# Hashed attention and a GELU feed-forward on one core: the second pair's feature transfers split between two queues, the weights' conversion shifted by one pair, the last accumulator in another PSUM bank

## The chip, the core and the metric

The kernel runs on one core of a Trainium2 chip. The metric is the device time of one execution in microseconds, the median of five runs. Beside it stands one profiled execution, with a record of every instruction of every engine; all times of single instructions below are from that execution, counted from its first instruction.

## What is computed

```python
q, k, v: (4, 8, 768, 64)     proj: (64, 6)     w_in: (512, 2048)     w_out: (2048, 512)
q_bits = (q @ proj > 0);  k_bits = (k @ proj > 0)        # 6 hash bits for each query and key
mask   = bucket(q_bits) == bucket(k_bits)
scores = where(mask, q @ k.T / 8, -1e9)
attn   = softmax(scores) @ v                             # (4, 8, 768, 64)
x      = attn.transpose(0, 2, 1, 3).reshape(3072, 512)
h      = x @ w_in
out    = (h / (1 + exp(-1.702 * h))) @ w_out             # (3072, 512)
```

All inputs and the output are float32; the two weights arrive as float64 and the kernel converts them bit by bit on the chip.

## The kernel before

**Two stages.** Attention takes about the first 328 us, the feed-forward the rest. The feed-forward multiplies by a block scheme with 7 products for 8 in two levels, so it needs sums of quarters of the weights (`in_sums`, on GpSimd) and of x (`x_sums`, on VectorE) before its first products. Four engines (TensorE, VectorE, ScalarE and GpSimd) execute in the order in which the program is written. SyncE only issues transfers; its order is chosen by the scheduler, which may move a transfer up past others when nothing it depends on holds it. Transfers signal through eight counters in turn, so an issue also waits for the transfer that used its counter before.

**Attention in pairs.** The 32 heads are handled as 16 pairs n = 0 to 15, two heads side by side in the 128 partitions. Each pair has two column halves c = 0 and 1 of 384 queries. One round of the main loop is one (n, c), called here by those numbers (pair 0 has its halves split once more). In a round TensorE computes `scores` of (n, c), six key tiles of 128, each with a masking product of the features `kf`, `qf` and a product of `kT`, `qT` (L432), into one of three two-bank PSUM buffers `ps`. ScalarE exponentiates each (L433), which frees its buffer. In the same round TensorE multiplies the round before's exponentials by the values (`values`, L456) into the accumulator `av`, which ScalarE unloads (L467, L468). `av` is one PSUM bank of the pool `aps`, and a second one-bank pool `mps`, tag "m", holds in turn the hashes, the denominators `dn` and the row of `guard`.

**Preparing the next pair.** In the rounds with c = 0 VectorE transposes the next pair's k and q as they have come from memory (`turn`, L391), ScalarE takes their squares' sum (`measure`, L398), TensorE hashes them (`hashed`, L408), and `featured` compares on VectorE (L413, tile `f`) and copies pieces of `f` into `kf` and `qf` by eight transfers of 9 KB (L420). For pair 1 four of these eight are issued by ScalarE and four by SyncE, for all others SyncE issues all eight. The raw k and q of a pair come in by eight transfers of 96 KB (`fetch`, L328) in pieces of 128 bytes.

**Denominators.** Exponentials are added up by GpSimd (`add_low`, L440, L441) and VectorE (`add_high`, L446, L448); TensorE sums over partitions (`total`, L477), VectorE inverts (`invert`, L484 to L492) and scales (`norm`, L497).

**Weights' conversion.** `w_in` comes in 16 chunks of 512 KB (L162, tile `raw`, one buffer). Fourteen are converted inside attention, one for a pair, two in the feed-forward. A conversion has three VectorE steps in the round with c = 0 (L178, L182, L186), one ScalarE step (L190, square), and three VectorE steps in the round with c = 1 (L193, L195, L198). `begin(n)` starts the generator and issues its load at the end of round (n-1, 1).

**The end of attention.** `guard(0)` reduces the sizes to one column on VectorE (L520), `guard(1)` turns it on TensorE (L523, tile `row`, in the bank "m") and reduces the row on VectorE (L524). In the kernel before, `guard(0)` stands in round (15, 1) and `guard(1)` after the last `values`.

Of the kernel before, what the change touches and what calls it, by code (L numbers as in the profile page):

```python
# [8 lines left out]
F32 = mybir.dt.float32  # L9
# [10 lines left out]
P = 128  # L20
# [18 lines left out]
def kernel(  # L39
# [17 lines left out]
    nc = tc.nc  # L57
# [10 lines left out]
    HS = HT * P  # L68
# [84 lines left out]
    for x in (0x3FFFFFFF, 0xFF800000):  # L153
        m = const.tile([P, 1], U32, name=f"mask_{x:x}")
# [3 lines left out]
    def convert(cv, dst, src, queue=None, psum=None):  # L158


        raw = cv.tile([P, CW, 2], U32, tag="raw", name="raw")
        (queue or loader[0]).dma_start(out=raw, in_=src)  # L162

        def of(x):
            return x if len(dst.shape) == 2 else x.rearrange("p (x r) -> p x r", r=dst.shape[2])

        lo, hi = raw[:, :, 0], raw[:, :, 1]
        bits = cv.tile([P, CW], U32, tag="bits", name="bits")
        if psum is None:
            part, size = dst.bitcast(U32), hi.bitcast(F32)  # L170
        else:
            part = psum.tile([P, CW], U32, tag="part", name="part")
            size = psum.tile([P, CW], F32, tag="size", name="size")
        yield


        if psum is None:
            nc.vector.scalar_tensor_tensor(part, hi, 3, masks[0x3FFFFFFF], op0=Alu.logical_shift_left, op1=Alu.bitwise_and)  # L178
        else:
            nc.vector.tensor_scalar(part, hi, 3, 0x3FFFFFFF, op0=Alu.logical_shift_left, op1=Alu.bitwise_and)  # L180
        yield
        nc.vector.scalar_tensor_tensor(bits, hi, 0xC0000000, part, op0=Alu.bitwise_and, op1=Alu.bitwise_or)  # L182
        yield

        if psum is None:
            nc.vector.tensor_tensor(part, bits, masks[0xFF800000], op=Alu.bitwise_and)  # L186
        else:
            nc.vector.tensor_scalar(part, bits, 0xFF800000, None, op0=Alu.bitwise_and)

        nc.scalar.activation(size, hi.bitcast(F32), Act.Square)  # L190
        part = part.bitcast(F32)
        yield
        nc.vector.scalar_tensor_tensor(part, lo, 2.0**-52, part, op0=Alu.mult, op1=Alu.mult)  # L193
        yield
        nc.vector.tensor_tensor(dst, of(bits.bitcast(F32)), of(part), op=Alu.add)  # L195
        yield

        nc.vector.scalar_tensor_tensor(dst, of(size), (1.125 * 2.0**-15) ** 2, dst, op0=Alu.is_ge, op1=Alu.mult)  # L198
# [3 lines left out]
    in_chunks = [(w_in_sb[:, kc, f : f + CW], wi[kc, :, f : f + CW])  # L202
                 for f0 in range(0, FF // 2, CW) for f in (f0, FF // 2 + f0) for kc in range(KC)]


    LATE = 2
# [76 lines left out]
    def attention(ff):  # L283
# [4 lines left out]
        with actx:  # L288
            ld = actx.enter_context(tc.tile_pool(name="ld", bufs=1))
            wk = actx.enter_context(tc.tile_pool(name="wk", bufs=2))  # L290
            cv = actx.enter_context(tc.tile_pool(name="cv", bufs=1))
            st = actx.enter_context(tc.tile_pool(name="st", bufs=2))
            aps = actx.enter_context(tc.tile_pool(name="aps", bufs=1, space=PSUM))
            mps = actx.enter_context(tc.tile_pool(name="mps", bufs=1, space=PSUM))
# [93 lines left out]
            def turn(n, name):  # L388
                x = raws[n, name]
                xt = xts[n, name] = wk.tile([P, S], F32, tag=f"{name}T", name=f"{name}T")  # L390
                nc.vector.transpose(xt, x.rearrange("p s i -> p (s i)"))  # L391
# [19 lines left out]
            def featured(n):  # L411
                f = wk.tile([P, HS], BF16, tag="f", name="f", bufs=1)
                nc.vector.tensor_scalar(f, dots.pop(n), above[:, 0:1], weight[:, 0:1], op0=Alu.is_gt, op1=Alu.mult)  # L413
                for c in range(2):
                    for i, x in enumerate("kq"):

                        queue = nc.scalar if (n, x) == (1, "q") else nc.sync
                        for j in range(2):
                            r0 = D * i + 32 * c + 2 * NB * j
                            queue.dma_start(out=feats[n % 2][x][D * j : D * j + 2 * NB, c * HS : (c + 1) * HS],  # L420
                                            in_=f[r0 : r0 + 2 * NB, :])
# [13 lines left out]
            accs, avs = {}, {}  # L435

            def add_low(n, c):

                acc = accs[n, c, 0] = st.tile([P, 2, HS], F32, tag="acc0", name="acc0", bufs=1)
                nc.gpsimd.tensor_tensor(acc, es[c][:, 0, :, 0:HS], es[c][:, 1, :, 0:HS], op=Alu.add)  # L440
                nc.gpsimd.tensor_tensor(acc, acc, es[c][:, 2, :, 0:HS], op=Alu.add)  # L441
# [7 lines left out]

            def values(n, c, kts):  # L450
                if 0 in kts:
                    avs[n, c] = aps.tile([P, HS + 1], F32, tag="av", name="av")
                av, vt = avs[n, c], vts[n]
                for t in kts:
                    for j in range(2):
                        nc.tensor.matmul(av[D * j : D * (j + 1), :], vt[:, t, j, :], es[c][:, t, j, :],  # L456
                                         start=(t == 0), stop=(t == T - 1))
# [37 lines left out]
            def norm(n):  # L495
# [4 lines left out]
            groups = [(n, c, kts) for n in range(len(pairs)) for c in range(2)  # L500
                      for kts in ((range(GT), range(GT, T)) if n == 0 else (range(T),))]
            last = len(pairs) - 1
            conv = {}

            def step(n, count=1):
                for _ in range(count):
                    next(conv.get(n, iter(())), None)

            def begin(n):
                if n - 1 < len(in_chunks) - LATE:  # L510

                    conv[n] = convert(cv, *in_chunks[n - 1], nc.sync if n > 1 else nc.scalar)
                    step(n)


# [2 lines left out]
            def guard(part):  # L518
                if part == 0:
                    nc.vector.tensor_reduce(largest, sizes, axis=AX.X, op=Alu.max)  # L520
                else:
                    row = mps.tile([1, P], F32, tag="m", name="row")
                    nc.tensor.transpose(row, largest, ident)  # L523
                    nc.vector.tensor_reduce(largest[0:1, 0:1], row, axis=AX.X, op=Alu.max)  # L524
# [7 lines left out]
            for g in range(len(groups) + 2):  # L532
                n, c, kts = groups[g] if g < len(groups) else (last + 1, 0, ())
                prev = groups[g - 1] if 1 <= g <= len(groups) else None
                if kts:
                    scores(n, c, kts)
                    if g == 0:
                        rest()
                    if kts[0] == 0:
                        add_low(n, c)  # L540


                if hashes:
                    featured(hashes.pop())
                ended = prev and prev[2][-1] == T - 1
                if ended:
                    add_high(*prev[:2])
                    if prev[1] == 1:
                        totals.append((g + (g == len(groups)), prev[0]))

                turned = ("", "k", "q", "")[g] if n == 0 else "kq" if c == 0 and n < last else ""
                for x in turned:
                    turn(n + 1, x)
                    measure(n + 1, x)
                while norms:
                    norm(norms.pop(0))
                if totals and totals[0][0] == g:
                    norms.append(totals.pop(0)[1])
                    total(norms[-1])
                    invert(norms[-1])  # L560
                if prev:
                    values(*prev)
                if ended:
                    unload(*prev[:2])
                if "q" in turned:
                    hashed(n + 1)
                    if n:
                        hashes.append(n + 1)
                    else:
                        featured(n + 1)  # L570
                    for x in "kq":
                        if n + 2 <= last:
                            fetch(n + 2, x)
                    fetch_v(n + 1)
                if kts and kts[-1] == T - 1:
                    step(n, 3)
                    if c == 0 and n > last - len(x_sums):
                        x_sums[n - last - 1]()
                    if c == 1:
                        begin(n + 1)  # L580
                if g == len(groups) - 1:
                    guard(0)
                if g == len(groups):
                    guard(1)
                    for f in in_sums(0):
                        f()
                    early.close()
                    next(ff)
# [410 lines left out]
```

## Time and profile before

| | |
|---|---|
| median of 5 runs | 884.34 us (884.04 to 884.95) |
| profiled execution | 884.37 us, span from first to last instruction 882.5 us |
| granted TensorE clock | 0.996 |
| busy, share of the span | TensorE 866.5 us (98%), VectorE 724.5 us (82%), ScalarE 313.4 us (36%), GpSimd 320.3 us (36%) |
| chain that ended last | 97% TensorE |
| TensorE waits on another engine | ScalarE exponential 2.5 us in 2 waits, unload of `av` 0.9 us in 1, later unloads 1.0 us in 2 |

The busy rows count the time in which an engine had an instruction under way. The chain is followed back from the last instruction to what released it, so its shares say which engine set the time. A timeline row reads: start, duration, engine, line, operation, output<-inputs, count; in brackets the idle time before it and what ended that. Rows marked SPq and ACTq are the issuing of transfers by SyncE and ScalarE.

### The profile page before, as it was taken

The numbers are of one execution on the slowest core, as the hardware profiler recorded it, in microseconds if no ns is written. First come the engines' busy times: TensorE is split into PE (matmuls) and PEld (weight loads), VectorE is DVE, ScalarE is ACT, GpSimd is POOL, SyncE is SP. The second block draws the span as 40 slices with busy tenths as digits, with TensorE's granted clock in tenths as the row PEclk, the third lists the DMA queues.
The fourth block names the chain that finished last, engine by engine and source line by source line (L and its number), as shares of the span: only waits on it lengthen the run. The fifth ranks groups of instructions, "written<-read, shape, count | busy, mean of one in ns | idle before, by whom it ended". The sixth has DMA issues, their size and how long they took to land.

```text
span 882.5 us, 11926 instructions
## 1 busy us (share of the span) xinstructions
PE 866.5 (98%) x4077; PEld 497.4 (56%) x4077; DVE 724.5 (82%) x1020; ACT 313.4 (36%) x519; POOL 320.3 (36%) x275
## 2 busy tenths in 40 slices
PE   9899999999999999999999999999999999999995
PEld 4444444444444444444444444444888888888884
DVE  4599999999999956777777887888898977897785
ACT  5666677667667732223222223322000000000000
POOL 4244334333433363775433444559932000000000
PEclk9999999999999999999999999999999999999998
DMA  4654554566444103555456545575835665467524
GB/s 103 116 90 83 86 102 81 96 101 101 85 83 83 46 1 131 202 196 188 165 193 213 198 166 200 185 247 180 306 140 190 207 212 208 158 217 239 191 96 99
DMA packets 169477, 132.01 MB, mean 150 GB/s; under 512 B 123936, under 2 KB 138432, under 8 KB 164032
## 3 DMA queue, kind: packets, MB, share of 16 engines
q1 hardware_dynamic: 167712, 129.69, 51.2%
q10 hardware_dynamic: 1696, 1.48, 0.6%
q8 instruction: 34, 0.56, 0.3%
q14 instruction: 35, 0.29, 0.1%
HBM read 79.69 MB, written 50.33 MB: 147 GB/s over the span
## 4 chain that ended last, share of the span: by engine, by line
PE 97%; DVE 1%; DMA 0%; ACTq 0%; ACT 0%; issue 0%; SPq 0%; DVEq 0%
PE product L699 33%; PE product L812 28%; PE ps L432 18%; PE av L456 14%; PE dn L477 2%; PE hash L408 1%; DMA pj<-in_proj_dram 0%; ACTq L420 0%; DVE xT L816 0%; PE hash L373 0%; DVE y L791 0%; ACT e L433 0%; PE tp L366 0%; DVE qf L374 0%; ACT xT L468 0%
## 5 line engine op out<-in xcount | busy, mean ns | idle before, releaser
L433 ACT ACTIVATE e<-ps 128x768 f32<-128x768 f32 x192 | 151.0, 812 | 18.4 <-PE ps L432 12.4
L432 PE MATMUL ps<-qT,kT 64*128 64x384 f32 x768 | 155.1, 482 | 0.0
L699 PE MATMUL product<-xT,w_in_sb 128*128 128x512 f32 x288 | 135.4, 592 | 0.0
L456 PE MATMUL av<-e,v 128*64 128x385 f32 x768 | 131.8, 490 | 0.9 <-ACT xT L468 0.9
L440 POOL TENSOR_TENSOR acc<-e 128x768 f32<-128x768 f32 x32 | 58.7, 1833 | 192.9 <-DVE acc L448 170.2
L707 ACT ACTIVATE c<-c 128x512 f32<-128x512 f32 x72 | 45.3, 630 | 186.2 <-issue 78.6
L456 PEld LDWEIGHTS av<-e,v 128*64 128x64 f32 x768 | 52.1, 136 | 77.6 <-issue 76.1
L699 PEld LDWEIGHTS product<-xT,w_in_sb 128*128 128x128 f32 x288 | 54.6, 190 | 68.5 <-issue 63.5
L699 PE MATMUL product<-t_x,s_in 128*128 128x512 f32 x192 | 90.2, 592 | 0.0
L432 PEld LDWEIGHTS ps<-qT,kT 64*128 64x128 f32 x768 | 68.2, 188 | 34.9 <-issue 34.8
L219 POOL TENSOR_TENSOR v<-c,u 128x512 f32<-128x512 f32 x24 | 34.2, 1423 | 127.6 <-ACT c L707 127.6
L818 ACT COPY u<-product 128x256 f32<-128x256 f32 x21 | 7.8, 372 | 167.9 <-PE product L812 125.7
L432 PE MATMUL ps<-qf,kf 64*128 64x384 bf16 x384 | 63.1, 324 | 2.7 <-ACT e L433 2.5
L699 PEld LDWEIGHTS product<-t_x,s_in 128*128 128x128 f32 x192 | 36.5, 190 | 45.9 <-issue 43.8
L441 POOL TENSOR_TENSOR acc<-acc,e 128x768 f32<-128x768 f32 x32 | 59.1, 1846 | 2.5
L699 PE MATMUL product<-xT,s_in 128*128 128x512 f32 x96 | 45.1, 592 | 0.0
L699 PE MATMUL product<-t_x,w_in_sb 128*128 128x512 f32 x96 | 45.1, 592 | 0.0
L432 PEld LDWEIGHTS <-kf 64*128 64x128 bf16 x384 | 19.1, 94 | 44.6 <-issue 23.1
L446 DVE SCALAR_TENSOR_TENSOR acc<-e 128x768 f32<-128x768 f32 x32 | 30.5, 954 | 7.7 <-ACT e L433 7.7
L467 ACT COPY vs<-av 128x1 f32<-128x1 f32 x32 | 5.1, 159 | 87.1 <-PE av L456 87.1
L812 PE MATMUL product<-raw_g,xT 128*128 128x256 f32 x152 | 35.1, 379 | 0.0
L448 DVE TENSOR_TENSOR acc<-acc,e 128x768 f32<-128x768 f32 x32 | 32.0, 999 | 3.3
(207 smaller groups left out, 1542.5 us busy)
## 6 DMA issues: line engine op xcount, KB each, us to landing
raw_g<-g_dram SPq DMA_DIRECT2D x22, 1024.0 KB
s_in<-g_dram SPq DMA_DIRECT2D x20, 1024.0 KB
g_dram<-c SPq DMA_DIRECT2D x72, 256.0 KB
g_dram<-t SPq DMA_DIRECT2D x48, 256.0 KB
raw<-in_moe_w_out_dram SPq DMA_DIRECT2D x16, 512.0 KB
raw<-in_moe_w_in_dram SPq DMA_DIRECT2D x15, 512.0 KB
v<-in_v_dram SPq DMA_DIRECT2D x32, 192.0 KB
g_dram<-u SPq DMA_DIRECT2D x24, 256.0 KB
```

What stands on the lines that cost most here:

```text
L219: return [lambda: eng.tensor_tensor(t1, b12, b11, op=Alu.subtract), lambda: eng.tensor_tensor(b12, b22, b12, op=Alu.subtract), lambda: eng ...
L432: nc.tensor.matmul(ps[:, j, 0:HS], a[hs, keys], m[hs, cols], start=not last, stop=last)
L433: nc.scalar.activation(es[c][:, kt, :, 0:HS], ps[:, :, 0:HS], Act.Exp, scale=1.0 / D**0.5)
L440: nc.gpsimd.tensor_tensor(acc, es[c][:, 0, :, 0:HS], es[c][:, 1, :, 0:HS], op=Alu.add)
L441: nc.gpsimd.tensor_tensor(acc, acc, es[c][:, 2, :, 0:HS], op=Alu.add)
L446: nc.vector.scalar_tensor_tensor(acc, e[0], T * TINY, e[1], op0=Alu.add, op1=Alu.add)
L448: nc.vector.tensor_tensor(acc, acc, x, op=Alu.add)
L456: nc.tensor.matmul(av[D * j : D * (j + 1), :], vt[:, t, j, :], es[c][:, t, j, :], start=(t == 0), stop=(t == T - 1))
L477: nc.tensor.matmul(dn[r0 : r0 + 32, :], ones[:, 0:32], acc[:, j, :], start=True, stop=True)
L699: nc.tensor.matmul(ps, wq[LEFT[i]][:, kc, :], xq[RIGHT[i]][:, kc, :], start=(kc == 0), stop=(kc == K2 - 1))
L707: nc.scalar.activation(c, c, Act.Gelu_apprx_sigmoid)
L812: nc.tensor.matmul(ps, wq[LEFT[i]][:, c, :], gq[RIGHT[i]][:, c, :], start=(c == 0), stop=(c == F4 - 1))
```

## The change

1. Of pair 1's eight feature transfers ScalarE issues two (q's, c = 0) instead of four; q's two of c = 1 go to SyncE.
2. `begin(n)` converts chunk n-2 instead of n-1, for n = 2 to 15 instead of 1 to 14, so pair 1 has no conversion and pair 15 has one. The first chunk's load is issued by SyncE instead of ScalarE. In the changed program's order it stands on SyncE sixth, right after pair 0's values and ahead of pair 1's k.
3. The last accumulator, `av` of (15, 1), is in the bank "m". So that the row of `guard` is not between it and its use there, `guard(0)` moves to round (15, 0) and `guard(1)` to the end of round (15, 1), after its conversion steps and ahead of the last `values`.

```diff
-                        queue = nc.scalar if (n, x) == (1, "q") else nc.sync
+                        queue = nc.scalar if (n, x, c) == (1, "q", 0) else nc.sync
...
             def values(n, c, kts):
                 if 0 in kts:
-                    avs[n, c] = aps.tile([P, HS + 1], F32, tag="av", name="av")
+                    pool, tag = (mps, "m") if (n, c) == (last, 1) else (aps, "av")
+                    avs[n, c] = pool.tile([P, HS + 1], F32, tag=tag, name="av")
...
             def begin(n):
-                if n - 1 < len(in_chunks) - LATE:
-                    conv[n] = convert(cv, *in_chunks[n - 1], nc.sync if n > 1 else nc.scalar)
+                if 0 <= n - 2 < len(in_chunks) - LATE:
+                    conv[n] = convert(cv, *in_chunks[n - 2])
                     step(n)
...
                     if c == 1:
                         begin(n + 1)
-                if g == len(groups) - 1:
-                    guard(0)
+                if g in (len(groups) - 2, len(groups) - 1):
+                    guard(g - len(groups) + 2)
                 if g == len(groups):
-                    guard(1)
                     for f in in_sums(0):
```

## The prediction

> **What bounds the kernel now.** First the chain of the page, then TensorE's waits and its timeline around each. The chain says that TensorE sets the time:
>
> ```profile
> PE 97%; DVE 1%; DMA 0%; ACTq 0%; ACT 0%; issue 0%; SPq 0%; DVEq 0%
> ```
>
> So only a stretch in which TensorE stands still can be won. Inside attention three such stretches follow its start (number before the bracket: start; in the bracket: idle time before it):
>
> ```profile
> 29.91 0.34 PE L432 MATMUL ps<-qf,kf 64*128 64x384 bf16 x2 [1.19 <-ACT e L433]
> ...
> 42.44 0.34 PE L432 MATMUL ps<-qf,kf 64*128 64x384 bf16 x2 [1.32 <-ACT e L433]
> ...
> 323.90 4.10 PE L456 MATMUL av<-e,v 128*64 128x385 f32 x24 [0.87 <-ACT xT L468]
> ```
>
> Together 3.38 us, 0.38%: no gain of this change can be larger. ScalarE's timeline tells why it was late in the first two:
>
> ```profile
> 24.94 3.87 ACTq L420 DMA_DIRECT2D qf<-f  x4
> 28.85 0.81 ACT L433 ACTIVATE e<-ps 128x768 f32<-128x768 f32 x1 [4.33 <-issue]
> ...
> 41.03 0.67 ACT L190 ACTIVATE raw<-raw 128x512 f32<-128x512 f32 x1 [2.04 <-DVE bits L182]
> ```
>
> It spent 3.87 us issuing four transfers, and it waited 2.04 us for VectorE's conversion steps before the exponentials of (1, 1). The third stop is the one accumulator bank: the last `values` waits for its unload.
>
> **Part 1, two issues fewer on ScalarE.** The first two take 1.58 and 0.74 us in the chain in order of time, ending at 27.29, so the exponentials start at 27.3 instead of 28.85, and the first ends at 28.1. TensorE is free at 28.72 (26.56 + 2.16). The stop of **1.19 us goes**. Next late would be the features themselves; the landing event of ScalarE's second transfer is at 28.41 in the trace, 0.3 us early, and the issue of these two does not change.
>
> The row shows 3.87 us for four transfers of 9 KB. The Trainium skill, "DMA: Bandwidth & Descriptors", section "Issuing engines are not separate DMA queues", says that the choice of issuing engine saves only the sequencer's time, usually small beside the transfer. By that rule this stop would hardly move and the time would come out near 884.5 us; the row decides here.
>
> On SyncE two issues are added, ahead of pair 2's last piece of k and its whole q:
>
> ```profile
> 24.92 3.30 SPq L420 DMA_DIRECT2D kf<-f  x4
> 28.27 0.70 SPq L328 DMA_DIRECT2D k<-in_k_dram  x1
> 29.30 3.64 SPq L328 DMA_DIRECT2D q<-in_q_dram  x4
> ```
>
> Two more at 0.74 (SyncE's later pairs of L420 take 1.47) push k to 29.7 and q to about 30.2. Pair 2's hash needs qT and the denominators' transpose, 1.5 us after q's landing (35.95 to 37.4 in VectorE's rows), and TensorE reaches it at 37.74 - 1.19 = 36.55: q must land by 35.05. Lower bound: as pair 1's q, four issues in 2.02 us and landed within 2.3 us (the DMA share falls to 0.04 in the window from 14 to 16, last issue 11.77), so 34.5, nothing lost. Upper bound: as this q before, 6.65 us from first issue to the end of VectorE's wait, so 36.9, 1.9 us lost. I take the lower: what slowed it, the 512 KB load issued by ScalarE at 28.93, is no longer there.
>
> **Part 2, no conversion in pair 1.** ScalarE no longer waits for VectorE at 41.03; the exponentials of (1, 1) follow the unload that ends at 39.0, less 1.19, before their third buffer is wanted. **1.32 us goes**; pair 2 had a conversion before and no stop, and meets VectorE no later than it did. A gain above that is excluded, since nothing else stops TensorE there; a loss would need VectorE later, and it has six steps fewer.
>
> The chunk's load moves from 28.93 to about 3.7, ahead of pair 1's k. At the 325 GB/s of the window from 4 to 6 us, 512 KB takes 1.6 us. Pair 1's k is issued by 8.24; with the longest landing seen (3.0 us, pair 2's q) and these 1.6 it is there at 12.8, and VectorE turns it at 14.65. Its cover is 1.8 us, cost nothing; without cover each us costs one. q has 5 us of cover (19.70).
>
> **Parts 2 and 3 at the end.** `av` of (15, 1) no longer waits for the unload, but in the bank "m" it comes after `row`, so TensorE now waits for the reduction of that row on VectorE, and this stands behind pair 15's conversion. How long these steps take shows in pair 14, which has them, with GpSimd's rows beside:
>
> ```profile
> 299.46 0.96 DVE L448 TENSOR_TENSOR acc<-acc,acc 128x768 f32<-128x768 f32 x1
> 300.34 0.95 DVE L497 TENSOR_TENSOR xT<-xT,rs 128x768 f32<-128x768 f32 x1
> 301.21 2.03 DVE L193 SCALAR_TENSOR_TENSOR w_in_sb<-raw,w_in_sb 128x512 f32<-128x512 uint32 x1
> 303.28 2.05 DVE L195 TENSOR_TENSOR w_in_sb<-bits,w_in_sb 128x512 f32<-128x512 f32 x1
> 305.43 0.69 DVE L198 SCALAR_TENSOR_TENSOR w_in_sb<-raw,w_in_sb 128x512 f32<-128x512 f32 x1
> ```
>
> ```profile
> 300.57 2.12 POOL L440 TENSOR_TENSOR acc<-e 128x768 f32<-128x768 f32 x1 [7.97 <-DVE acc L448]
> 302.77 2.01 POOL L441 TENSOR_TENSOR acc<-acc,e 128x768 f32<-128x768 f32 x1
> ```
>
> L193 takes 2.03 beside GpSimd's additions; in the feed-forward, where its other operand is in PSUM, 0.70. And pair 15 before:
>
> ```profile
> 310.06 0.58 DVE L484 STREAM_TRANSPOSE rt<-dn 128x384 f32<-128x384 f32 x1 [0.94 <-PE dn L477]
> ...
> 312.87 1.18 DVE L222 TENSOR_TENSOR t_x<-xT,t_x 128x1024 f32<-128x1024 f32 x1
> ...
> 320.24 2.25 DVE L448 TENSOR_TENSOR acc<-acc,e 128x768 f32<-128x768 f32 x1
> 322.59 1.30 DVE L448 TENSOR_TENSOR acc<-acc,acc 128x768 f32<-128x768 f32 x1
> ```
>
> VectorE waited 0.94 us for `dn`, so its clock restarts at 310.06 in the old count. Inversion to 312.87; three new steps 2.02 (as 293.60 to 295.62), 314.9; sum of x 1.11, 316.0; `guard(0)` 0.1; additions 2.98 (313.98 to 316.96), 319.1; norm, L193 and L195 5.09 (300.34 to 305.43), 324.2; L198 0.61; the reduction 0.28: 325.06. Behind GpSimd's additions `in_sums` (L211) now follows at once, and beside L211 the addition at 322.59 took 1.30 instead of 0.96; I add 0.34 for L198: 325.4. TensorE ends the values of (15, 0) at 323.03 and waits until 325.45 instead of 323.90: **1.55 us lost**; `row` moves into that wait and gives back 0.10 (327.94 to 328.04). Net **+1.45**. Bounds: with L193 and L195 at 0.70 there is no wait at all, -0.97; with L198 at 2.03 like them, +2.45. I take the rows of the same steps in the same place.
>
> The rows show VectorE and GpSimd lengthening each other. The Trainium skill, "SBUF — State Buffer", section "Who interferes with whom", goes further: of a VectorE instruction with two SBUF inputs and a GpSimd instruction that reads SBUF, the second waits for the whole of the first. By it L198 would wait for all of L211 (0.72 us) and the sum would be 883.7 us.
>
> Behind this, ScalarE's square (0.66) delays the exponentials of (15, 1) from 315.07 to 315.5; the first then ends at 316.3, before its buffer is wanted at 316.41: nothing. GpSimd is 2 us later with the sums that the second product needs, its fourth and last step done by 329 (325.2 before and 2 to 3.5 later) against 331: nothing. The feed-forward shifts as a whole.
>
> **Sum**, from the profiled execution's own 884.37: 884.37 - 1.19 - 1.32 + 1.45 = 883.31. That execution is 0.03 over the median, so 883.3.
>
> **Rivals.**
> - *The end costs little.* If GpSimd and VectorE fall otherwise and L193 and L195 run at 0.70 each, the reduction is done at 322.7: 884.37 - 3.38 - 0.10 = 880.9; halfway, with the old 0.87 left, 881.9. Against it: all 14 conversions in attention have L193 at 1.98 to 2.04.
> - *Pair 2's q is late (slower).* Two issues and the fetch share SyncE; if the fetch is as slow as before, q lands at 36.9, TensorE waits 1.9 at the hash: 885.2. It decides from 35.05 on, and outweighs the gains from 36.1. Each us later costs one more, and 886.1 is reached at 37.9. For it: VectorE waited 1.41 for this q before. Against it: the load that shared its time is gone.
> - *The first stop only changes its name.* If the features land later than 28.41 the stop at 28.72 stays in part: up to 884.5. For it: the time given as wait for ScalarE can hide one for a transfer that ended sooner.
>
> **How the numbers follow.** As forecast 0.57, with its own range 882.4 to 884.4 (L198 from unhindered to 2.03 us, and half a us more or less in the early part); the end costs little 0.25; q late 0.10; stop renamed 0.08. About what a measurement of this kernel can tell from no change is 0.2%, 1.77 us: faster is below 882.57, slower above 886.11. Faster: the first rival, 0.25, and 0.06 of the forecast's low end. Slower: 0.04 of the second rival, for a fetch slower still than before, and 0.02 for a stop that no row shows. Range 881.6 to 885.2: it leaves out the deep end of the first rival and the far end of the second.
>
> **What would show it.** Right: no idle over 0.2 us in TensorE's rows between 20 and 300 us; one before the last `values`, near 2.4 us, ended by VectorE's second reduction of `guard`; L198 of pair 15 at about 1 us. Wrong: a stop at pair 2's hash ended by VectorE after a DMA wait; the reduction done before TensorE's values of (15, 0) end.

## The result and the profile after

The changed kernel takes 886.66 us (median of 25 executions, 884.56 to 888.97) against 884.58 us of the kernel before beside it (45 executions): a ratio of 1.0022, 95% interval 1.0017 to 1.0028. So it is 2.1 us slower, where 1.0 us faster was forecast, and the time lies above the range. The profiled execution took 886.19 us, its span is 884.4 us and its mean granted clock 0.994 (0.996 before). Its lines answer to those shown of before; `values` is now L458, `guard`'s second reduction L525, the transpose of `dn` L486.

The chain that ended last, from the page:

```profile
PE 95%; DVE 3%; DMA 1%; ACTq 0%; ACT 0%; issue 0%; SPq 0%; DVEq 0%
```

Two shares of the chain have left TensorE, 2% of the span to VectorE and 1% to a transfer. The timeline shows where; these rows are of ScalarE, SyncE, VectorE and TensorE, in order of time:

```profile
24.73 2.34 ACTq L420 DMA_DIRECT2D qf<-f  x2
27.11 2.21 ACT L433 ACTIVATE e<-ps 128x768 f32<-128x768 f32 x3 [2.80 <-PE ps L432]
...
30.24 2.21 SPq L328 DMA_DIRECT2D q<-in_q_dram  x4
...
36.92 0.98 DVE L391 STREAM_TRANSPOSE qT<-q 128x768 f32<-128x768 f32 x1 [3.80 <-DMA q<-in_q_dram]
...
38.41 0.52 PE L408 MATMUL hash<-kT,pf_k 128*32 128x384 f32 x2 [2.08 <-DVE rt L486]
...
324.00 5.80 PE L458 MATMUL av<-e,v 128*64 128x385 f32 x24 [2.26 <-DVE largest L525]
```

The exponentials start at 27.11 and both early stops (1.19 and 1.32 us) are gone. In their place stands a stop of 2.08 us at pair 2's hash: VectorE waited 3.80 us for q. At the end TensorE waits 2.26 us, and then the last values take 5.80 us instead of 4.10. VectorE's rows ahead of that last wait:

```profile
318.49 2.04 DVE L193 SCALAR_TENSOR_TENSOR w_in_sb<-raw,w_in_sb 128x512 f32<-128x512 uint32 x1
320.56 2.06 DVE L195 TENSOR_TENSOR w_in_sb<-bits,w_in_sb 128x512 f32<-128x512 f32 x1
322.72 1.02 DVE L198 SCALAR_TENSOR_TENSOR w_in_sb<-raw,w_in_sb 128x512 f32<-128x512 f32 x1
323.67 0.27 DVE L525 TENSOR_REDUCE largest<-row 1x1 f32<-1x128 f32 x1
```

The table by stretches tells why the values were slow. The first columns are the stretch, its length and TensorE's busy time; the third number from the end is the granted clock:

```profile
322.00:324.00 2.00, 0.00 (x1) 0.00 (x1) 1.90 (x4) 0.36 (x1) 1.92 (x3) 1.00 0.00 0
324.00:326.00 2.00, 2.00 (x8) 0.82 (x10) 1.90 (x2) 0.00 (x0) 1.92 (x3) 0.63 0.00 0
326.00:328.00 2.00, 2.00 (x8) 0.73 (x6) 1.84 (x2) 0.00 (x0) 2.00 (x2) 0.52 0.02 4
328.00:330.00 2.00, 2.00 (x13) 0.85 (x10) 0.00 (x0) 0.16 (x1) 1.92 (x3) 1.00 0.00 0
```

TensorE did as good as nothing from 322 to 324, and then its clock was halved: by the clock's records from 324.52 to 327.94, 3.41 us. The same 24 products took 1.70 us more.

**The balance**, from TensorE's idle times and rows in the two profiled executions: -1.19 and -1.32 for the early stops, +2.08 at the hash, +1.39 at the end (2.26 for 0.87), +1.70 for the halved clock, -0.10 for `row` in the wait, -0.65 for pair 1's denominators (below), -0.2 at the start, where two short waits of q's transposes are missing. The sum is +1.7; the profiled executions differ by 1.82. Without the halved clock it would be 0.0: the lateness of q alone used up the gain that was forecast.

### The profile page after: what moved, and what is told of

It is laid out like the page before. It is cut to its first block, busy times and chain, and to the rows that moved or that the text cites. A ratio compares the mean times of both kernels' runs of the same rounds, so it can differ in the third digit from the quotient of the medians.

```text
span 884.4 us, 11922 instructions
## 1 busy us (share of the span) xinstructions
PE 867.9 (98%) x4077; PEld 498.8 (56%) x4077; DVE 726.4 (82%) x1020; ACT 313.0 (35%) x519; POOL 321.7 (36%) x275
## 4 chain that ended last, share of the span: by engine, by line
PE 95%; DVE 3%; DMA 1%; ACTq 0%; ACT 0%; issue 0%; SPq 0%; DVEq 0%
PE product L699 33%; PE product L812 28%; PE ps L432 17%; PE av L458 13%; PE dn L479 1%; PE hash L408 1%; DMA q<-in_q_dram 1%; PE tp L366 1%; DVE acc L448 0%; DVE xT L816 0%; PE warm L359 0%; PE hash L373 0%; ACTq L420 0%; DVE y L791 0%; DVE w_in_sb L195 0%
## 5 line engine op out<-in xcount | busy, mean ns | idle before, releaser
L458 PE MATMUL av<-e,v 128*64 128x385 f32 x768 | 133.5, 496 | 2.3 <-DVE largest L525 2.3
L458 PEld LDWEIGHTS av<-e,v 128*64 128x64 f32 x768 | 52.6, 137 | 79.7 <-issue 77.2
```

## The experiments

Each run stands beside executions of the kernel before: 884.58 us in the first four experiments, 885.00 in the next four, 885.15 in the last three. The "program-code transfer" of theory A is a DMA packet of 16 KB; the rows that show it stand under "The row a step earlier".

**Part 1 alone**, on the kernel before:

```diff
-                        queue = nc.scalar if (n, x) == (1, "q") else nc.sync
+                        queue = nc.scalar if (n, x, c) == (1, "q", 0) else nc.sync
```

> The kernel before with the first part alone: two of pair 1's feature transfers from ScalarE instead of four, two more from SyncE. Theory A (pair 2's q is late because a sixteenth of its last piece lies behind TensorE's program-code transfer, which comes when TensorE reaches that place in its program): the first stop (1.19 us at 29.91) goes, the code transfer comes 1 to 2 us earlier and meets q, q lands at 36.9 or later, and TensorE stands 2 us or more at pair 2's hash; the second stop (1.32 us, conversion) stays or grows less than it, so 884.6 - 1.2 + 2 + about 0 = 885.0 to 886.0. Rival B (the two added issues push q back by 1.5 us and nothing else): q lands at about 37.4 in place of 35.95, hash stop about 1.3 to 2.4, so the same sign; the two are told apart by whether fifteen sixteenths of q have landed long before the last one. No slow clock in either, 884.6 to 885.8.

Measured: 885.56 us, ratio 1.0008 (0.9999 to 1.0017), within the forecast but not clear of no change. TensorE's waits in its timeline:

```profile
38.74 0.52 PE L408 MATMUL hash<-kT,pf_k 128*32 128x384 f32 x2 [2.08 <-DVE rt L484]
43.74 0.34 PE L432 MATMUL ps<-qf,kf 64*128 64x384 bf16 x2 [1.61 <-ACT e L433]
```

The stop of 1.19 us is gone, the one at the hash is there without the other parts, and the second early stop grew from 1.32 to 1.61. So part 1 moves the first stop to a later place and makes it longer. A transfer lands in 16 shares: of q's last piece 14 had landed by 35.79 us, the other two at 36.67 and 37.22, as theory A has it.

**Part 2 alone**: on the kernel before, only `begin` as in the change.

```diff
-                if n - 1 < len(in_chunks) - LATE:
-                    conv[n] = convert(cv, *in_chunks[n - 1], nc.sync if n > 1 else nc.scalar)
+                if 0 <= n - 2 < len(in_chunks) - LATE:
+                    conv[n] = convert(cv, *in_chunks[n - 2])
```

> The kernel before with the second part alone: conversions in pairs 2 to 15, first chunk's load early on SyncE. Theory A: ScalarE still issues four, so TensorE keeps the stop of 1.19 us and reaches the place of its code transfer as late as before (35.3 or later); q is issued at 28.3 to 32 without the 512 KB load beside it and lands by 34.5, the second stop of 1.32 us goes: 884.6 - 1.3 = 883.3. The end as before (stop 0.87 for the unload, full clock), because the last accumulator stays in its own bank. Rival B expects the same here; a time over 884.2 would say that the shift itself costs something at the end or at the start.

Measured: 882.39 us, ratio 0.9976 (0.9967 to 0.9986). The one stop left early is the first, 1.19 us. q is issued first at 28.84 and has landed by 34.03, and VectorE doesn't wait for it:

```profile
34.05 0.98 DVE L391 STREAM_TRANSPOSE qT<-q 128x768 f32<-128x768 f32 x1
```

The gain is larger than the 1.32 us stop, 2.2 us. Of the rest 0.65 us is a wait that hid in a busy row: pair 1's denominators took 1.50 us before, since their later products waited for VectorE's sums, and take 0.85 here (the rows of the changed kernel, which shows the same, stand under "A gain not seen").

**Part 3 alone**: on the kernel before, `av` of (15, 1) in the bank "m" and `guard` moved as in the change. No conversion stands in pair 15 then.

> The kernel before with the third part alone: last accumulator in the bank of the hashes, both steps of guard one round earlier, no conversion in pair 15. Theory C (at the end TensorE stands because the reduction of the row lies behind pair 15's conversion, and this idle time makes the clock drop to a half for 3.4 us): here the reduction has no conversion ahead of it, so no idle time over 0.2 us, full clock, last values 4.10 us: 884.6 - 0.97 = 883.6. Rival D (the bank or the order itself makes the last values slow, 5.80 us): 883.6 + 1.7 = 885.3.

Measured: 884.31 us, ratio 0.9995 (0.9986 to 1.0004). The last stop fell from 0.87 to 0.37 us and the last values ran in 4.10:

```profile
323.63 4.10 PE L457 MATMUL av<-e,v 128*64 128x385 f32 x24 [0.37 <-DVE largest L525]
```

The bank does not make the values slow. Theory C asked for no idle time over 0.2 us and for 883.6: TensorE makes the row only at 322.99 here, behind the values of (15, 0), and then waits for the reduction of 0.28 us.

**The row a step earlier**, on the changed kernel: `guard(1)` ahead of the conversion steps of round (15, 1) instead of behind them.

```diff
+                if g == len(groups) - 1:
+                    guard(1)
...
-                if g in (len(groups) - 2, len(groups) - 1):
-                    guard(g - len(groups) + 2)
+                if g == len(groups) - 2:
+                    guard(0)
```

> The changed kernel with the second step of guard (row) moved ahead of the values of (15, 0), so that its reduction comes ahead of pair 15's last three conversion steps; the conversion stays in pair 15. Theory C: no idle time before the last values and no slow clock: the changed kernel's 886.7 less 2.26 less 1.7 = 882.7, with the stop of 2.1 us at pair 2's hash unchanged. Rival D: last values still 5.80 us, 884.4.

Measured: 882.86 us, ratio 0.998 (0.9971 to 0.9989), 3.8 us under the changed kernel. All 48 products of values run through, at full clock:

```profile
316.66 0.27 PE L524 MATMUL row<-ident,largest 128*1 128x128 f32 x1
316.86 7.99 PE L458 MATMUL av<-e,v 128*64 128x385 f32 x48
```

So the wait and the slow values both came from the row standing behind the conversion. What stays is the stop at the hash, 1.79 us. The next question was why q is late. In these traces the transfer records show, beside q's, one packet of 16 KB on an instruction queue. Such packets recur some 260 TensorE instructions apart, from which it is taken for TensorE's program code; no record names it. In the changed kernel, from 33 to 36 us (packets, MB, share of the 16 DMA engines):

```profile
q1 hardware_dynamic: 2650, 0.51, 99.5%
q8 instruction: 1, 0.02, 2.8%
q14 instruction: 1, 0.01, 0.6%
```

The one of 16 KB is on q8 and runs from 33.75 to 35.10; the one on q14 has 8 KB. Of the 16 shares of q's last piece 14 landed by 35.05, the others at 35.76 and 36.90. The last 48 packets of 128 bytes run only from 35.08 to 35.82, that is from the end of the 16 KB packet on. That is 65 in a us, where some 1230 in a us had run before (31.0 to 33.75): about the share of one of the 16 DMA engines. So they are taken to have waited behind the 16 KB packet on its engine; the records do not name a packet's engine. In the kernel before, the 16 KB packet came at 35.78, q's packets having ended at 34.79.

**The 16 KB packet moved, first try**: the changed kernel with 24 more TensorE instructions at the start.

```diff
-                for _ in range(4):
-                    nc.tensor.matmul(aps.tile([P, 512], F32, tag="av", name="warm"), idle[:, 0:P], idle, start=True, stop=True)
+                for _ in range(16):
+                    nc.tensor.matmul(aps.tile([P, P], F32, tag="av", name="warm"), idle[:, 0:P], idle[:, 0:P], start=True, stop=True)
```

> The changed kernel, except that the idle multiplications at the start are 16 of 128 columns instead of 4 of 512: the same columns in all, 24 more TensorE instructions (12 products, 12 weight loads). The 16 KB program-code transfer that follows TensorE's instruction count then comes some 4 us earlier, near 29.5 instead of 33.75, before pair 2's q is under way. Theory A (one sixteenth of q lies behind that transfer): q lands near 34.8, the stop at pair 2's hash falls from 2.08 us to at most 0.4, the end is unchanged with its 2.26 us stop and slowed last values, and the time is 886.66 - 1.8 = 884.9. Theory B (the two issues added to SyncE alone make q late): the stop stays at 2.0 and the time at 886.7.

Measured: 886.97 us, ratio 1.0025 (1.0014 to 1.0036). The shorter products took 5.09 us instead of 2.53, so everything came 2.4 us later. Against the program the packet came only 2.1 us earlier and fell into the middle of q's transfer instead of ahead of it; the fourth issue of q took 1.78 us instead of 0.56. The hash stop fell to 1.03 us, which neither theory had said: not decided. But the last wait was 2.25 us long as before, and this time the clock stayed full:

```profile
325.36 4.11 PE L458 MATMUL av<-e,v 128*64 128x385 f32 x24 [2.25 <-DVE largest L525]
```

**The same with the row earlier**: both edits together.

> The kernel of row_early with the same 16 shorter idle multiplications. Theory A: no stop over 0.4 us between 20 and 325 us, so row_early's 882.86 less its hash stop of 1.8: 881.1; and no stretch at half clock, as no idle time is left that could bring one. Theory B: hash stop 1.8 stays, 882.9.

Measured: 884.45 us, ratio 0.9995 (0.9986 to 1.0003). No stop at the end; the features' copies 3.75 us later than in the trace of the earlier row (27.97 for 24.22); the 16 KB packet again inside q's transfer, the hash stop 1.30 us. Missed for the same reason, and no version to keep.

**Parts 2 and 3 with the earlier row, without part 1**: the kernel of the earlier row, with ScalarE's four issues as before.

```diff
-                        queue = nc.scalar if (n, x, c) == (1, "q", 0) else nc.sync
+                        queue = nc.scalar if (n, x) == (1, "q") else nc.sync
```

> Parts 2 and 3 of the change with the row of guard a step earlier, and without part 1: ScalarE issues its four transfers as in the kernel before. First stop 1.19 us as before, no second, no hash stop (q's issues on SyncE start as early as before), no stop at the end. p2_shift's 882.39 less the last stop of 0.87 and the row's 0.10: 881.4. If part 2 alone (and not part 1) made q late, the hash stop of about 2 comes back: 883.4.

Measured: 881.67 us, ratio 0.996 (0.9947 to 0.9973), as expected within 0.3 us. One stop over 0.2 us between the start and 600 us, the first early one, 1.19 us. q is issued first at 29.11 here and has landed at 34.68, before the 16 KB packet at 35.38.

**The whole program later**: the changed kernel with 8 idle multiplications of 512 columns instead of 4.

> The changed kernel with 8 idle multiplications of 512 columns instead of 4, which puts what follows up to 2 us later against the first instruction and brings the code transfer 8 instructions (about 1.3 us) earlier against the program. Stops: hash 2.08 less at most 1.3, end 2.26 as before. Theory C (the half clock follows 2.26 us of idle wherever they fall in one interval of 3.41 us): last values slow in some executions and not in others, as the place of the grid against the program differs; their row is either 4.1 or near 5.8. Rival D (the bank of the hashes makes the values slow): 5.8 always. Time between 886.7 - 1.3 + 0 and 886.7 + 2.

Measured: 888.35 us, ratio 1.0035 (1.0022 to 1.0048). The start cost 2.6 us. Hash stop 1.50 us, last wait 2.25, last values 5.80 us: slowed again, so this run alone does not tell theory C from its rival.

**The 16 KB packet moved, second try**: one idle multiplication of 512 columns and 60 of 32, 114 TensorE instructions more.

```diff
-                for _ in range(4):
-                    nc.tensor.matmul(aps.tile([P, 512], F32, tag="av", name="warm"), idle[:, 0:P], idle, start=True, stop=True)
+                nc.tensor.matmul(aps.tile([P, 512], F32, tag="av", name="warm"), idle[:, 0:P], idle, start=True, stop=True)
+                for _ in range(60):
+                    nc.tensor.matmul(aps.tile([32, 32], F32, tag="av", name="warm"), idle[:, 0:32], idle[:, 0:32], start=True, stop=True)
```

> The changed kernel, except that the idle multiplications are one of 512 columns and 60 of 32 columns with 32 weight columns, 114 more TensorE instructions. Everything behind them starts some us later (a constant, read off the first transposes of k), and the second program-code transfer comes before the feature copies instead of inside pair 2's q. Theory A+ (about half of the late landing is the 1.4 us later issue, the rest is the share behind the code transfer): q lands 5.2 us after its first issue, as in p2_shift, instead of 6.66, and the stop at pair 2's hash is 0.3 to 0.7 us. Theory B (the issue alone): the stop stays at 1.0 or more. The end: 2.25 us stop as before; last values 4.1 or 5.8 by the place of the clock's intervals. The median only tells the added start.

Measured: 897.38 us, ratio 1.0137 (1.0122 to 1.0153); everything comes 13.05 us later, which is the added start. The packet ran from 42.28 to 43.38, before q's first packet at 43.84. In the transfer records from 44 to 49 us there is none of 16 KB, only one of 8 KB on q14:

```profile
q1 hardware_dynamic: 5169, 0.82, 97.5%
q14 instruction: 1, 0.01, 0.7%
```

The timeline of SyncE, VectorE and TensorE (one line number higher):

```profile
43.29 2.45 SPq L328 DMA_DIRECT2D q<-in_q_dram  x4
...
48.66 0.98 DVE L392 STREAM_TRANSPOSE qT<-q 128x768 f32<-128x768 f32 x1 [2.50 <-DMA q<-in_q_dram]
...
50.16 0.52 PE L409 MATMUL hash<-kT,pf_k 128*32 128x384 f32 x2 [0.77 <-DVE rt L487]
...
335.73 4.10 PE L459 MATMUL av<-e,v 128*64 128x385 f32 x24 [2.24 <-DVE largest L526]
```

q needed 5.35 us from first issue to landing (48.64), not 6.66, and the stop is 0.77 us. Theory B, the issue alone, asked for 1.0 or more. So of the 2.08 us about 1.3 went with the packet, and 0.77 stays, which is put down to the issue: it comes 1.40 us later than in the run of part 2 alone. Theory A+ fits, its 0.7 a little low. This is one trace, but in all seven traces with the issue as late as this and the packet inside q's transfer the stop is 1.03 to 2.08 us.

**The changed kernel once more**, for a second trace:

> The changed kernel once more, for a second trace of it. Stops 2.1 at the hash and 2.25 at the end. Theory C: with the clock's intervals laid out in steps of 3.413 us from the first rise to full clock, the last values take 5.8 us if at least 2.2 us of the end's idle time lie in one interval, and 4.1 if 2.0 us or less do (2.26, 2.20: slowed; 2.02: not, in the three traces so far). Rival: the place does not matter, and the same 2.25 us slow them in one execution and not in another.

Measured: 886.0 us; hash stop 1.79, last wait 2.25, last values 5.80 us. The clock rose to full at 6.08, so one of its intervals runs from 320.11 to 323.52, and the wait (321.11 to 323.36) lies inside it. All changes of the granted clock within a trace lie a whole number of times 3.413 us apart, and this is how the five traces with such a wait come out:

| kernel | idle before the last values | of it in one interval | last values |
|---|---|---|---|
| changed, profiled | 2.26 us | 2.26 | 5.80 us |
| changed, again | 2.25 | 2.25 | 5.80 |
| whole program later | 2.25 | 2.20 | 5.80 |
| packet moved, first | 2.25 | 2.02 | 4.11 |
| packet moved, second | 2.24 | 1.30 | 4.10 |

The stops at the hash, at most 1.76 us of them in one interval, halved no clock in any trace. Counted over every interval of all thirteen traces, from the first rise to full clock on: each in which TensorE was busy for 1.21 us or less was followed by half clock, and none with 1.40 us or more was. And the kernel of "packet moved, first" is hit in some executions only: two of its seven had a mean clock of 0.994 and took 888.1 and 888.8 us, the others 0.995 to 0.997 and 886.0 to 887.2. The place decides, as theory C has it.

**A version to keep**: the kernel of the earlier row, with the two q copies of c = 1 issued by GpSimd.

```diff
-                        queue = nc.scalar if (n, x, c) == (1, "q", 0) else nc.sync
+                        queue = nc.sync if (n, x) != (1, "q") else nc.gpsimd if c else nc.scalar
```

> A version meant to keep what worked: the conversion a pair later, the last accumulator in the bank of hashes with guard's row a step earlier, and of pair 1's q copies two issued by ScalarE and the other two by GpSimd, which has nothing to do from 24.5 to 32.2 us; SyncE's queue is as in the kernel before. If SyncE's later issue was half of the lateness: no first stop, q issued near 28.9 and landed by 34.1 to 35.5 (the code transfer may still meet its last piece), hash stop 0 to 0.7, no end stop: 880.5 to 881.2 us, at or below p2_row's 881.67. If GpSimd's issues take long, the first stop comes back under another name: 881.7 or more.

Measured: 881.16 us (880.56 to 882.03), ratio 0.9954 (0.994 to 0.9967): 4.0 us under the kernel before beside it, and 5.5 under the changed kernel's 886.66. GpSimd and VectorE:

```profile
25.72 1.34 POOL L420 DMA_DIRECT2D qf<-f  x2 [0.49 <-DVE v L315]
...
34.92 0.98 DVE L391 STREAM_TRANSPOSE qT<-q 128x768 f32<-128x768 f32 x1 [1.51 <-DMA q<-in_q_dram]
```

The two issues take GpSimd 1.34 us of a stretch in which it had nothing to do, q's packets ended at 33.71, ahead of the 16 KB packet (34.54), and TensorE has no idle time over 0.2 us between its start and 600 us. Against the version without part 1 it won only 0.5 us of the 1.19, and their ranges overlap. In its trace the start was some 0.6 us later, which may be the rest; that is not shown for the medians.

## Why the prediction was wrong

**Right.** Both early stops went, and ScalarE's exponentials started at 27.1 as worked out. That the first stop "only changes its name" by late features did not happen. The end's mechanism and size were right: 2.26 us of wait for 2.42, ended by `guard`'s second reduction, L193 and L195 at 2.04 and 2.06, L198 at 1.02 where about 1.0 was said. The rule from the Trainium skill, "SBUF — State Buffer", section "Who interferes with whom", that L198 would wait for the whole of L211, is not what this trace shows: L211 runs from 322.03 for 1.17 us, and L198 starts inside it, at 322.72; both take longer than alone (1.02 for 0.69, 1.17 for 0.72). The rule on issuing engines in "DMA: Bandwidth & Descriptors", section "Issuing engines are not separate DMA queues", holds here in one half: what another engine's issuing saved is the issuer's own time, 3.87 us down to 2.34. "Usually small" does not fit: these 1.53 us had held up the exponentials (28.85, now 27.11) and cost TensorE the whole first stop.

**The step that failed first** is the landing of pair 2's q, whose cost the sum put at nothing; it cost 2.08 us. The issue was forecast right (30.2, measured 30.24), the bounds were 34.5 and 36.9, and the lower was taken because the 512 KB load was gone. The upper came, 36.90, and with it the rival "pair 2's q is late" at its price (1.9 us forecast, 2.08 measured). That it came so close is luck: the 6.65 us of the upper bound were those of a transfer beside the 512 KB load, and here the 16 KB packet took as long in its place. The reason for the lower bound was half right: without that load q takes 5.19 us (part 2 alone) and 5.57 us (parts 2 and 3 with the earlier row) instead of 6.63. But 5.2 from 30.24 is 35.4, already past the 35.05 that was needed. And the 16 KB packet, which had followed this transfer before, now fell into it: the issue came 0.9 us later (30.24 for 29.30), and the packet 2.0 us earlier (33.75 for 35.78), since TensorE, without its first stop, was sooner at the same place of its program (some 450 instructions in both). Pair 1's q, which took 4.22 us from first issue to landing, was the wrong row to take: this q's own issues and landings, and what ran beside them, were in the trace.

**The step that was missing** is the clock. The forecast counted some 2.4 us of idle time at the end and priced it at itself; in the trace it cost 1.70 us more. That made the end +2.99 instead of +1.45, and with the hash the total. It does not happen in every execution: 3 of the 25 of the changed kernel had a mean granted clock of 0.996 and took 884.6 us, 2.1 under the median; all others had 0.994 or 0.995 but for three at 0.992. The 884.6 us is the kernel before's own time, as the balance without the halved clock says. A stretch of 3.41 us at half clock is 0.002 of the span's mean, so the steps fit one such stretch and two; that the second one would follow the stop at the hash was not seen in a trace, but the kernel of the earlier row, which has no wait at the end, had one execution of 11 at 0.994 too (884.49 us, 1.6 over its median). Why 22 of 25 executions are hit stays open: with the intervals placed at random against the program, 2.2 of 2.26 us would fall in one in about 4 cases of 10 (an estimate from the lengths: (3.41 - 2.26 + 2 x 0.06) / 3.41 = 0.37).

**A gain not seen** is the 0.65 us in pair 1's denominators. No idle time of TensorE shows it: the wait is inside a row of eight products that counts as busy, 1.50 us against 0.85. VectorE and TensorE before, then TensorE after:

```profile
53.60 0.96 DVE L448 TENSOR_TENSOR acc<-acc,acc 128x768 f32<-128x768 f32 x1
53.96 1.50 PE L477 MATMUL dn<-acc,ones 128*32 128x384 f32 x8
...
53.13 0.85 PE L479 MATMUL dn<-acc,ones 128*32 128x384 f32 x8
```

Before, the sum that the later four products need ends at 54.56, inside the row. So the prediction's limits do not hold, 3.38 us for the whole change and 1.32 for part 2: part 2 alone won 2.2 us, and the version to keep 4.0.

## What to carry to other kernels

Before an issue is moved later on a queue, look up not only what is queued behind it but what else runs on the DMA engines at the new time, the program-code transfers too; take the bound from the same transfer's own rows, and from a neighbour's only if nothing stands between. A new wait of TensorE of over 2 us is priced with the slower products behind it as well as with itself. And a step that VectorE can do early for a later TensorE product (here the row of `guard`) belongs ahead of long work on VectorE, not behind it.

## What the hardware showed

- A wait of TensorE with 2.20 us or more in one interval of 3.41 us was followed by the next 3.41 us at half clock in three traces; one with 2.02 us or less there was not, in two. The Trainium skill, "TensorE: Matmul & The Clock Gate", section "Why this matters for your kernels", advises no idle gaps over about 3 us between bursts; here a gap of 2.25 us sufficed.
- A 16 KB packet on an instruction queue held up a small part of a transfer of 128-byte pieces, by its rate about a sixteenth: the landing of q took 1.3 us longer with it than without it (6.66 and 5.35 us).
- Two transfers issued by an idle GpSimd took 1.34 us, about what SyncE took for two (1.48), and less than ScalarE's 2.34 beside it.
